# Pooled attention and a max-out MoE in one program: loads without a wait for an earlier load, and a new order of all engines and loads

## The chip, the core and the metric

The kernel runs on one core of a Trainium2 chip. TensorE (PE), ScalarE (ACT), VectorE (DVE) and GpSimd (POOL) each work through their own instructions in program order; SyncE (SP) issues nearly all of the DMAs, also in order, and 16 DMA engines carry them out. The metric is the device time of one execution in microseconds, the median of several.

## What is computed

```python
def _attn_ref(q, k, v):                       # 8 batches, 8 heads, 1152 positions, head size 64
    q_pool = q.reshape(B, H, S // 2, 2, D).mean(axis=3)
    scores = 1.0 / np.sqrt(D) * np.matmul(q_pool, k.transpose(0, 1, 3, 2))
    scores = scores - np.max(scores, axis=-1, keepdims=True)
    attn = np.exp(scores)
    attn = attn / (np.sum(attn, axis=-1, keepdims=True) + 1e-09)
    return np.matmul(attn, v)

def _moe_ref(x, w1, w2, w_out):               # x: 4608 tokens x 512; w1, w2: 512 x 1024; w_out: 1024 x 512
    g = np.maximum(x @ w1, x @ w2)
    return g @ w_out
```

The attention's output, heads side by side, is the `x` of the second part. Inputs and output are float32; the kernel multiplies in bfloat16.

## The kernel before

The 64 heads go in 32 pairs of two; a pair's q, k and v are three loads of 576 KB each. For each pair q is pooled and cast (`cast_q`, L435, on POOL), k is cast (`cast_k`, L405, POOL), v is cast and given a column of ones (`cast_v`, L445, POOL). k and q are turned so that the head size lies on the partitions: for pairs 0 to 4 on PE with a copy by DVE (`ktrans_pe`, L552 and L568; `qtrans`, L533 and L540), from pair 5 on k by a DMA transpose that SP issues (`ktrans`, L475), and q by eight small transposes on DVE (`qtrans_dve`, L485).

Scores come in 324 groups of 512 columns for both heads of a pair (`scores`, L302, on PE, into a pair of PSUM banks); ACT takes the exponent of each group (`exps`, L317; 336 instructions, since some groups are split where a buffer turns). A pair has 10.125 groups, so pair 3 begins in group 30, pair 4 in group 40, pair 6 in group 60. The product with v (`av_jobs`, L621 and L636, letter A) has eight steps a pair with a few more for the remainders, and DVE divides by the sums (L651, L654). The result is turned into `xT`.

The MoE uses max(a, b) = relu(a - b) + b. So the kernel forms `wd` = w1 - w2 on POOL, in eight halves of quarters (`w_diff`, L506), and the fused weight `w21` = w2 w_out on PE (`w_job`, L593), for which w2 is cast and turned and w_out is cast on DVE (`w_cast`, L498). The steps of relu(x wd) are `h_jobs` (L760, and L771 or L775 for the way out of PSUM), those of the output are `p_job` (L803, and L809 or L812). All of these are the letters 0 and 1. The first of them, the fused weight's, begin as soon as its weights are there; then come the first that read `wd`.

The order of the work is written out by hand as a string of letters, one letter a step, that a loop passes to `step`; it fixes the order on each engine and, with S for scores and E for exponents, how far the engines are apart. `BANKS` names the PSUM banks in that order. `LOADS` is the order of the loads (letter l takes the next one on SP; four small pieces of k of pair 0 and two of q of pair 0 come first, two of them on ACT's queue), `W_CASTS` that of the weight casts (letter c), `W_DIFFS` that of the halves of `wd` (letter d; the pair is quarter and half). In `LOADS` ("w", 0, c) is quarter c of w2, ("w", 1, c) of w1 and ("w", 2, c) of w_out; each is 512 KB.

Every step names what it reads and writes, and `Plan` puts in the semaphore waits that follow. A load waits for its buffer: there are three for each of q, k and v. From exponent 40 on it also waits for the exponent two groups back (`pace`). And by `BEHIND` it waits for an earlier load:

```python
        def behind():

            n = issued[0]
            issued[0] += 1
            back = [d for at, d in BEHIND if at <= n]
            return [f"ld{n - back[-1]}"] if back else [], [f"ld{n}"]
```

With `BEHIND = ((14, 3),)` the load at place 14 on SP (counted from 0) and all later ones wait until the load three places ahead has landed. `load_k`, `load_q`, `load_v` and `w_load` call it.

Of the kernel before, what the change touches and what calls it, by code (L numbers as in the profile page):

```python
# [116 lines left out]
def bass_funnel_attn__then__act_maxout2_kernel(  # L117
# [68 lines left out]
    BANKS = (
        "0124605424023623462032424660232342630240624702402064202420472042646264246024604640164604264126402406"
        "0240260240246304260346204040640606062061262062062402740264062402406402640642704260202402402406401640"
        "6460462056204620462046042164206204620620426026402602602602604604614646046046024604604204620420642040"
        "6406406742064264264206520640260462620620162062046206240620206204230642042042424126426046046045620642"  # L190
        "6024062046206206206206412640246056046206404024024026423236042642042626260262626426454526420642064206"
        "2454"
    )

# [1 line left out]
    with ctx:  # L196
# [230 lines left out]
        def cast_q0(i, lo, hi):  # L427
            op("DVE", lambda e: e.tensor_tensor(
                qpf[i][:, lo:hi, :], qraw[i][:, lo:hi, 0, :], qraw[i][:, lo:hi, 1, :], ALU.add),
                r=[f"qraw0.{lo}" if i == 0 else f"qraw{i}"], w=[f"qp{i}.{int(hi == QU)}"],  # L430
                cost=0.14 + (hi - lo) * 0.07, tag=("cq", i))
# [59 lines left out]
        def w_cast(part, ct, eng):  # L491
            n = 2 if part else 1
            src = (wof if part else w2f)[:, ct * n:(ct + 1) * n, :].rearrange("p a b -> p (a b)")
            dst = (wo if part else w2b)[:, ct * n:(ct + 1) * n, :].rearrange("p a b -> p (a b)")
            r = [f"wof{ct}" if part else f"w2f{ct}"]
            w = [f"wo{2 * ct}", f"wo{2 * ct + 1}"] if part else [f"w2b{ct}"]
            if eng == "DVE":
                op("DVE", lambda e: e.tensor_reduce(dst, src.unsqueeze(2), AX.X, ALU.max),  # L498
                   r=r, w=w, cost=1.21, tag=("wc", part, ct))
# [459 lines left out]
        for c in (
            "luFFlulllfyKQklgfbSkKEFlgFKSgESyFFlKEFgQSbESlFkSFEFFKlEySFSgESlqFFEFQlSbEFkSQElbKvSEgSlESceAAEATcESA"  # L960
            "EAhlkSaSEaASclEKAEglSAEcSAElvSaTaEhElTcSAESlAhAEScAElSSAcEAAlAqESa0a00aE0la0ScAE0SldQEaa00bSd0lEXSj0"
            "00ESvTl0h0E00eS4SlEAAkAEAlSa1ad1E1S1SEl1q1S1E1Kl1g1qE1S1SE1lQkrAEbArSdtAErArSE11avlEa1S5AElSdArESSrA"
            "dArEArSAEkAlaAaSEaAdatAESaXadjXEjSjSEXq0jl00jE0S0qr0E0lSr01rE11e41Sl1E1Sk1r10Er005St0ESv00r0ESSr0rvE"
            "lA4AAEASqalSaEAArAErAlSrSEEaAeaAArxAErSSaAEaAklrAAErS1at1ak1E1r0Sr0xE0r0Sr11E1rS1r0E050Sl0E0q0SrS0tE"
            "r01r10Er0eS0r0E0r0Skr0lE0r1S0r0E0rlSv0r1E14S11El1S1oSE1oAAEASAkEAaAlaSAEtAvSa1aE1SxS11ES111E1111ES11"
            "l1ESq5AAEAlSrSoEAroArAESrkSArEAaAalAEAaAaSvaaEtaSSrXEqArAjAEAjSrle00Ea0aS0rSE0lr0vSr0E1r01rlE114S11E"
            "1S1rSEA5AlvAEASr0E0ta0Eva0SrSE00xe00SE4AAkAESSlAEAaAaAEAlSa1aE1Sx000E0Sk11E0lS11E11S50qlE00tS00ESer0"
            "0rSE00rS0rE00r00Er0l0qSrSE0r01l1r0E14S11E1l1SroSE1r1o11roSErAoArAtEkArAAaaAArq1ESaa1E1Sx001r001E1r0S"
            "1rE0l001rS141E1rS1r1ES5AAEvAAroSSrvoESAlAAEvAaAaAlEAaAkaSa000SaEt0a000011114Ee111S111115E1S111Xl5EvS"
            "j00j0ESl0qSE0000SEl4AAAEArSSaEAaArAlqEArS1a1taE11rSESrE1e1xrS1r1EA5AAEASla0kaE0Sr00rSEq0l0r0SEr0ArAl"  # L970
            "E4SAAESr11aE1a1Srx1ESr11r1SEt5qAAAEArSe0aE0a0Slr0SEkr0S0r0E0lrS0r0E0r0Sl0rE0000ES0S0Er0tArAEArArS0aE"
            "0aq0Srx10Er1S14k1E1S11EroS1rSo1E1oAAoEvAAS1vElSAAlEAvAaSa1ESalAaAAEASa1aE1taS1rXvE1rS1j11Ej1eSrl11rE"
            "11qrSS5EAlAAkEAroS0a0oEa0S0rS0ErAAlAEASa0a0E0l0S4x00E0qSE0r00E0trSA4eAEAArS1a1Ea1k1Sr11ESr1lSr1E5AAA"
            "lEArS1a1Ea11Srx00E10S1l1E1S500tE0Sq0rS0Er00r0e0ESr00rSEl0kr00r0E0rS0l0ES00SE0A4AAEAAaAoaAoASaoSqaE11"
            "x11SESkr11t1rE11rE11rE1SrS1E1r11r1SEr11S1E1S11E1A5AEvAASoSvESlAAoAEvAaAaAElAaAa0Sa0a0E0taS00r0000E04"
            "e0Sx000r0E11141vS1x1E11r100500Sr11qE1Sr01lr110E1rS050E0Sl0r0E0SS0l0E0S0r0EArAArEAArlAkaAaArSE0etEa0a"
            "S0r0SE0rxS0rq0EA4AAEASkao1aE11o1SSE11lS11EA5AAElASa1aE1Sx0r00E0rS1rt0E0er0Sr0E1S4111ESl1r0q0E500S0lE"
            "0SrS0r0EA4lAAEAAAaaAASa1aESlk1Sx1r1ES1r11Ert11r11Er1qSSr1E1rArAEvAS1E11klS11El11vS1E1S1lvA5ESAAEAoAa"
            "oSaSESaAtaArAEArq00Ea0aSa00rExSv0r00ErS0xe0r0E0rSSr0kl0E0S00E0Sl00E0S00El0A4AEAAAaoSaSEoArAtArE00Ea0"
            "0aeS00rxE1111r00qS411E1111151S1k1E1r1Sl00500ESr000SrEl0A4AAEArSla1aE1S1S1EAAAEAlSa1aE1tSrS1rq1E1r1x1"  # L980
            "1rESSre11Er11rSk1Elr11S1E11Sl1E1A5AAEASaoSaEAoAAoEAoSa0a0tEq00rSESr0E00rx00k040E0AArvAArSrSvElArArAE"
            "AvaAaAAaAaSaSaE00a001x14E11S11E1x11Sv511E100S1SE0r1t11r0ES0500E0eSr00Er00SrSE0r00r0SEr0S00E0S00E0004"
            "0E00S0E0oS00oSE4AAAEAAaAaAeAAaEAaAAxAaAaAASa0aES0x00SE1000E0S411E1S11E111500S0E00S11E1S11E1S10E50S00"
            "E0S10E0Se10E00S00E0S00E0S00E10S41E11S11EoS11o1E1oSSo1E1AAEAAAaAaAAAaAaAxAAAAAaAaAAaAa1a1a1a11X1j11j1"
            "11111900001111111150000111o080110091o110000008101110191101000018111009101110000080101111191100000001"
            "001111910000000011111111110001000800110000o008001o11o00010181111Z9ZZZZZoZZoZZZZZZmZZZZzzZZZZZZZZZZmZ"
            "ZZZZZZzZzmzz"
        ):
            step(c)
# [52 lines left out]
```

## Time and profile before

| what | value |
|---|---|
| median of 3 runs | 365.27 us (364.27 to 365.68) |
| profiled execution | 362.49 us, span 360.8 us |
| PE clock granted, mean | 0.999 |
| loads of q, k, v: median from issue to landing | 6.2, 6.5, 5.8 us |
| DMA packets on SP's queue | 75856, 83.15 MB |

The profile is one execution on the chip. Its views name an engine, a line, the operation, and what is written and read; an idle time in front of an instruction carries the name of what ended it (`[1.91 <-PE ps L302]`: idle for 1.91 us until the matmul of line 302 was done). Matmuls are pipelined, so two that follow one another overlap in these lists, and the time from start to start is what one takes.

### The profile page before, as it was taken

How to read it: one execution, taken by the hardware profiler on the slowest of the kernel's cores; microseconds unless marked ns; L12 is line 12 of the kernel's file. 1: busy time of each engine (PE TensorE's matmuls, PEld its weight loads, DVE VectorE, ACT ScalarE, POOL GpSimd, SP SyncE). 2: the span in 40 equal slices, each digit the busy share in tenths (PEclk: the TensorE clock that was granted, in tenths of full speed). 3: DMA queues.
4: the chain of work that ended last, by engine and by line, in shares of the span. 5: the costliest groups of instructions: out<-in, count | busy, mean ns of one | idle time of the engine just before them, and what ended most of it. 6: DMA issues, size and time to landing. Idle time of an engine off the chain costs nothing.

```text
span 360.8 us, 13815 instructions
## 1 busy us (share of the span) xinstructions
PE 347.0 (96%) x6178; PEld 218.6 (61%) x6178; DVE 230.0 (64%) x472; ACT 314.0 (87%) x354; POOL 151.7 (42%) x136
## 2 busy tenths in 40 slices
PE   8888989999899999999999999999999999999996
PEld 6554564755655576556665576556575757448753
DVE  3587378992984985986886677785686875324001
ACT  5997979999999899999999889989999797892431
POOL 2623798562754444546444264326544531010000
PEclk9999999999999999999999999999999999999999
DMA  8999999999999989999999979999999972112215
GB/s 265 407 308 324 328 287 319 292 265 295 315 275 242 354 187 307 228 317 193 211 336 314 200 202 301 195 325 244 262 251 225 277 120 60 31 23 55 60 29 148
DMA packets 76699, 84.55 MB, mean 234 GB/s; under 512 B 48480, under 2 KB 49760, under 8 KB 76640
## 3 DMA queue, kind: packets, MB, share of 16 engines
q1 hardware_dynamic: 75856, 83.15, 88.2%
q8 instruction: 48, 0.79, 0.9%
q10 hardware_dynamic: 784, 0.52, 0.5%
q14 instruction: 11, 0.09, 0.1%
HBM read 62.91 MB, written 9.44 MB: 201 GB/s over the span
## 4 chain that ended last, share of the span: by engine, by line
PE 76%; DMA 12%; ACT 6%; DVE 2%; SPq 2%; issue 1%; POOL 1%; DVEq 0%; POOLq 0%
PE ps L803 23%; PE ps L621 17%; PE ps L302 16%; PE ps L760 15%; ACT et L317 6%; DMA kraw<-in_k_dram 5%; DMA qraw<-in_q_dram 3%; PE ps L636 3%; PE ps L846 1%; DMA stage<-in_moe_w_dram 1%; DMA stage<-in_moe_w_out_dram 1%; DMA vraw<-in_v_dram 1%; DVE qpT L485 1%; POOL qp L435 1%; SPq L346 1%
## 5 line engine op out<-in xcount | busy, mean ns | idle before, releaser
L317 ACT ACTIVATE et<-ps 128x1024 bf16<-128x1024 f32 (+1 forms) x336 | 302.5, 1019 | 18.6 <-PE ps L302 14.1
L302 PE MATMUL ps<-qpT,kT 64*128 64x256 bf16 (+7 forms) x1162 | 117.5, 283 | 4.8 <-DVE qpT L540 1.7
L485 DVE STREAM_TRANSPOSE qpT<-qp 32x288 bf16<-32x288 bf16 x216 | 101.3, 469 | 14.5 <-PE ps L302 6.2
L760 PE MATMUL ps<-xT,wd 64*128 64x512 bf16 (+3 forms) x832 | 81.2, 311 | 0.2
L302 PEld LDWEIGHTS ps<-qpT,kT 64*128 64x128 bf16 x1162 | 48.2, 94 | 52.4 <-ACT et L317 10.7
L803 PE MATMUL ps<-wo,stage 64*128 64x512 bf16 x544 | 76.4, 376 | 0.0
L435 POOL TENSOR_TENSOR qp<-qraw 128x576 bf16<-128x576 f32 x30 | 42.2, 1406 | 67.5 <-DMA qraw<-in_q_dram 67.5
L621 PEld LDWEIGHTS ps<-vE,et 128*128 128x128 bf16 x1728 | 54.8, 97 | 13.7 <-ACT et L317 8.9
L621 PE MATMUL ps<-vE,et 128*128 128x65 bf16 x1728 | 60.5, 193 | 0.5 <-ACT et L317 0.3
L771 DVE TENSOR_SCALAR stage<-ps 128x1024 bf16<-128x1024 f32 (+3 forms) x41 | 39.7, 968 | 20.7 <-PE ps L760 20.3
L760 PEld LDWEIGHTS ps<-xT,wd 64*128 64x128 bf16 x832 | 35.6, 94 | 22.3 <-PE ps L760 1.9
L405 POOL TENSOR_SCALAR kbf<-kraw 128x1152 bf16<-128x1152 f32 x31 | 35.8, 1153 | 31.1 <-DMA kraw<-in_k_dram 29.1
L803 PE MATMUL ps<-w,xT 64*128 64x512 bf16 x272 | 40.8, 377 | 0.0
L803 PEld LDWEIGHTS ps<-wo,stage 64*128 64x128 bf16 x544 | 26.4, 94 | 20.6
L445 POOL TENSOR_SCALAR vE<-vraw 128x1152 bf16<-128x1152 f32 x24 | 27.4, 1154 | 21.4 <-PE ps L636 10.7
L809 DVE COPY stage<-ps 128x1024 f32<-128x1024 f32 x14 | 17.1, 1224 | 22.9 <-PE ps L803 22.8
L654 DVE TENSOR_TENSOR xnat<-ps,rc 128x256 bf16<-128x256 f32 (+2 forms) x71 | 27.6, 397 | 2.0
L651 DVE RECIPROCAL rc<-ps 128x4 f32<-128x4 f32 (+2 forms) x64 | 11.6, 181 | 25.8 <-PE ps L621 25.2
L468 POOL TENSOR_SCALAR stage<-et 128x1152 bf16<-128x1152 bf16 x14 | 16.1, 1153 | 28.1 <-ACT et L317 28.1
L621 PE MATMUL ps<-stage,et 128*128 128x65 bf16 x576 | 19.8, 193 | 0.4 <-issue 0.4
L621 PEld LDWEIGHTS ps<-stage,et 128*128 128x128 bf16 x576 | 18.2, 97 | 3.2 <-issue 3.1
L803 PEld LDWEIGHTS ps<-w,xT 64*128 64x128 bf16 x272 | 12.5, 94 | 8.8 <-DVE stage L771 0.2
(55 smaller groups left out, 155.7 us busy)
## 6 DMA issues: line engine op xcount, KB each, us to landing
vraw<-in_v_dram SPq DMA_DIRECT2D x32, 576.0 KB, 5.8
kraw<-in_k_dram SPq DMA_DIRECT2D x31, 576.0 KB, 6.5
qraw<-in_q_dram SPq DMA_DIRECT2D x31, 576.0 KB, 6.2
...
```

Source lines behind the costliest of these rows:

```text
L302: last = e.matmul(ps[:, h, col:col + hi - lo], kT[i % 3][rows(h), t, :], qpT[i % 3][rows(h), lo:hi], start=True, stop=True)
L317: op("ACT", lambda e: e.activation(et2[:, :, c:c + z - a], ps[:, :, a - g * W:z - g * W], EXP, scale=scale), r=[f"b{m}", f"b{m + 1}"], w=w ...
L405: op("POOL", lambda g: g.tensor_scalar(kbf[s][:, :, :, :].rearrange("p t h d -> p h t d"), kraw[r][:, :, :, :], 1.0, 1.0, ALU.mult, ALU.mu ...
L435: op("POOL", lambda g: g.tensor_tensor(qpf[s][:, :, :], qraw[r][:, :, 0, :], qraw[r][:, :, 1, :], ALU.add), r=[f"qraw{r}"], w=[f"qp{s}.0", ...
L445: return g.tensor_scalar(vE[r][:, :, :, 0:D].rearrange("p t h d -> p h t d"), vraw[s][:, :, :, :], 1.0, 1.0, ALU.mult, ALU.mult)
L485: op("DVE", lambda e: e.transpose(view[dst:dst + 32, :, 32 * pb:32 * pb + 32], qpf[s][src:src + 32, :, 32 * db:32 * db + 32]), r=[f"qp{s}. ...
L621: last = e.matmul(fb[m][:, at * 66:at * 66 + 65], et[:, a:a + P], vE[vs][:, t, half, 0:65], start=(t == 0), stop=(t == NT - 1))
L654: todo.append(evac_op("DVE", lambda e, m, z=z, at=at, num=num, dst=dst: e.tensor_tensor(dst, a(m)[z, at:at + num, 0:D], rc[k][z, at:at + n ...
L760: last = e.matmul(fb[m + k][:, 0:size], wd[z, ct, (f0 + k) * P:(f0 + k + 1) * P], xT[z, ct, n0:n1], start=(turn == 0 and ct == 0), stop=(t ...
L771: return e.tensor_scalar_max(gT[:, f0:f0 + 2, g0:g0 + size], wide[m // 2][:, :, 0:size], 0.0)
L803: last = e.matmul(fb[m + k][:, :], lhs, rhs, start=(turn == 0 and j == 0), stop=(turn == 1 and j == NC_ + NF - 1))
L809: return e.tensor_copy(osb2[:, o:o + 2, :], wide[m // 2][:, :, :])
```

## The change

`BEHIND` becomes empty, so no load waits for another one to land; the waits for buffers and exponents stay. The loads, the weight casts, the halves of `wd`, the PSUM banks and the order of all steps are replaced by others. No step is added or taken away: both strings have 2712 letters, and the same number of each. The loads' order differs up to about pair 16, and the order of the steps mostly up to the same place; behind it single letters have moved by a few places.

```diff
@@ -153,27 +153,27 @@
     X_PE = (0, 1, 2, 3, 7, 11, 15, 31)
     HCUTS = (0, 512, 1024, 1152, 1664, 2048, 2304, 2816, 3072, 3456, 3968, 4096, 4352, 4608)
     W_ORDER = (1, 2, 0, 3)
-    W_CASTS = ((0, 1), (0, 3), (0, 0), (0, 2), (2, 0), (2, 1), (2, 2), (2, 3))
-    W_DIFFS = ((3, 0), (3, 1), (1, 0), (2, 0), (2, 1), (0, 0), (0, 1), (1, 1))
+    W_CASTS = ((0, 1), (0, 0), (0, 2), (2, 1), (2, 0), (2, 2), (2, 3), (0, 3))
+    W_DIFFS = ((3, 1), (0, 1), (1, 0), (2, 0), (3, 0), (0, 0), (1, 1), (2, 1))
     W_DIFFS_DVE = ()
     W_CASTS_POOL = ()
     W_PAIRS = (0, 2)
-    BEHIND = ((14, 3),)
+    BEHIND = ()
     FILL = 28
     FILLS = 16
     PACE = 2
     PACE_FROM = 40
     FOUR = 1
     LOADS = (
-        ("k", 0, 0, 2, "ACT"), ("k", 0, 4, 6, "ACT"), ("q", 0, 0, 4), ("k", 0, 2, 4), ("k", 0, 6, 9),
-        ("q", 0, 4, 9), ("k", 1), ("q", 1), ("q", 2), ("k", 2), ("v", 0), ("w", 0, 1), ("w", 0, 3),
-        ("k", 3), ("w", 0, 0), ("w", 0, 2), ("v", 1), ("w", 2, 0), ("w", 2, 1), ("w", 2, 2), ("q", 3),
-        ("w", 2, 3), ("w", 1, 3), ("v", 2), ("w", 1, 2), ("k", 4), ("w", 1, 1), ("q", 4), ("q", 5),
-        ("k", 5), ("v", 3), ("w", 1, 0), ("k", 6), ("q", 6), ("q", 7), ("k", 7), ("v", 4), ("v", 5),
-        ("q", 8), ("k", 8), ("k", 9), ("k", 10), ("q", 9), ("v", 6), ("k", 11), ("v", 7), ("k", 12),
-        ("q", 10), ("v", 8), ("q", 11), ("v", 9), ("v", 10), ("v", 11), ("k", 13), ("k", 14), ("q", 12),
-        ("v", 12), ("q", 13), ("v", 13), ("k", 15), ("q", 14), ("v", 14), ("k", 16), ("v", 15),
-        ("q", 15), ("q", 16), ("v", 16), ("q", 17), ("k", 17), ("v", 17), ("q", 18), ("k", 18),
+        ("k", 0, 0, 2, "ACT"), ("k", 0, 4, 6, "ACT"), ("k", 0, 2, 4), ("q", 0, 0, 4), ("k", 0, 6, 9),
+        ("k", 1), ("q", 0, 4, 9), ("q", 1), ("q", 2), ("k", 2), ("v", 0), ("w", 0, 1), ("w", 0, 0),
+        ("v", 1), ("w", 0, 2), ("k", 3), ("w", 2, 0), ("w", 2, 1), ("w", 2, 2), ("w", 2, 3), ("w", 0, 3),
+        ("q", 3), ("w", 1, 3), ("k", 4), ("q", 4), ("v", 2), ("k", 5), ("w", 1, 0), ("v", 3), ("k", 6),
+        ("q", 5), ("w", 1, 1), ("w", 1, 2), ("k", 7), ("q", 6), ("v", 4), ("k", 8), ("q", 7), ("v", 5),
+        ("q", 8), ("q", 9), ("v", 6), ("q", 10), ("v", 7), ("v", 8), ("k", 9), ("v", 9), ("q", 11),
+        ("v", 10), ("k", 10), ("v", 11), ("k", 11), ("k", 12), ("v", 12), ("k", 13), ("v", 13),
+        ("k", 14), ("q", 12), ("q", 13), ("v", 14), ("q", 14), ("v", 15), ("q", 15), ("k", 15),
+        ("q", 16), ("k", 16), ("v", 16), ("q", 17), ("k", 17), ("v", 17), ("q", 18), ("k", 18),
         ("v", 18), ("q", 19), ("k", 19), ("v", 19), ("q", 20), ("k", 20), ("v", 20), ("q", 21),
         ("k", 21), ("v", 21), ("q", 22), ("k", 22), ("v", 22), ("q", 23), ("k", 23), ("v", 23),
         ("q", 24), ("k", 24), ("v", 24), ("q", 25), ("k", 25), ("v", 25), ("q", 26), ("k", 26),
...
@@ -184,11 +184,11 @@
         "wwhhhhpphhhhpphhhhhhhhpphhhhpphhhhphhhhpphhhhphhhhphhhhpphhhhhhhhhphphh"
     )
     BANKS = (
-        "0124605424023623462032424660232342630240624702402064202420472042646264246024604640164604264126402406"
...
+        "0101010102460625640647672606422026342046203406402462046206202024016240260420402406520462060526026046"
...
@@ -957,33 +957,33 @@
                  "m": ("Z", 0), "4": ("0", 0), "5": ("1", 0), "6": ("2", 0), "7": ("3", 0),
                  "8": ("0", 1), "9": ("1", 1), "+": ("2", 1), "-": ("3", 1)}
         for c in (
-            "luFFlulllfyKQklgfbSkKEFlgFKSgESyFFlKEFgQSbESlFkSFEFFKlEySFSgESlqFFEFQlSbEFkSQElbKvSEgSlESceAAEATcESA"
-            "EAhlkSaSEaASclEKAEglSAEcSAElvSaTaEhElTcSAESlAhAEScAElSSAcEAAlAqESa0a00aE0la0ScAE0SldQEaa00bSd0lEXSj0"
-            "00ESvTl0h0E00eS4SlEAAkAEAlSa1ad1E1S1SEl1q1S1E1Kl1g1qE1S1SE1lQkrAEbArSdtAErArSE11avlEa1S5AElSdArESSrA"
-            "dArEArSAEkAlaAaSEaAdatAESaXadjXEjSjSEXq0jl00jE0S0qr0E0lSr01rE11e41Sl1E1Sk1r10Er005St0ESv00r0ESSr0rvE"
-            "lA4AAEASqalSaEAArAErAlSrSEEaAeaAArxAErSSaAEaAklrAAErS1at1ak1E1r0Sr0xE0r0Sr11E1rS1r0E050Sl0E0q0SrS0tE"
-            "r01r10Er0eS0r0E0r0Skr0lE0r1S0r0E0rlSv0r1E14S11El1S1oSE1oAAEASAkEAaAlaSAEtAvSa1aE1SxS11ES111E1111ES11"
-            "l1ESq5AAEAlSrSoEAroArAESrkSArEAaAalAEAaAaSvaaEtaSSrXEqArAjAEAjSrle00Ea0aS0rSE0lr0vSr0E1r01rlE114S11E"
-            "1S1rSEA5AlvAEASr0E0ta0Eva0SrSE00xe00SE4AAkAESSlAEAaAaAEAlSa1aE1Sx000E0Sk11E0lS11E11S50qlE00tS00ESer0"
...
+            "ulFFluFFlFFlFFFlffklykKlQgKbgSFESlFkKKEggSFlSEyFFQEblSyFESSSlEFqKEgSlkEQSbQElKbvgESSlSEcSElAecAEAAlT"
+            "aEaAvAhSlEScSAAElaTakEShTlEhKSgSElSAcESlEcSEAEAlAcSEA00cl0E00S0E00lSc00E0SAlEq0aSa0a0E0a0lSd4SEQAlAE"
+            "bkAASaTaElqhSKESg11le1E1S11ESvl1S1EQk1lb1E11Sdt1E1SS11EvA5AAEAkSlaSaEAAtqAEASaESaAEdrArAESrSdrEXrAjd"
+            "ESrlSrErdAAElAaSakXaESaAljAdEAjSaXaElSdjXt1jE1Sj0q0E00S0E0Ser00r1E1lS4v11E1S1rSklE0500E0qS0lrSE0r0Ar"
+            "AElArArS0aESaAlvA4tAEASEeaSEaSArxAErAqArSEaAaAArEAvrS1la1Ea1Sr1x0E0r1Sr1E1rqS1rl00E50S00E0lSr00Er00S"
+            "rSlE0rvS0r00Er00ler00E0rSSrq0El0r10r1E114Slk1E11SroS1ErtAArAEAAoaSaq1ESArAAEr1aSa1E1rxSSr1k1E1r11rSE"
+            "t1r11r1ES111ES5AAEvASoSEAovAlAESSvAEAlaAaAEAaAaSlaSaESarXElAerAjAEAjSr0lv0EaSa00r1E1rlSk0r0E0rS0t1rE"
+            "1kS411E11S5SEAAlAEASa0aE0t0ESe0SE00x00ES4AAEASkSElAAaAaEAAlSa1aE1Sx000E0Sk11E0Sl11E11S50lE0Sq0t00ES1"
...
```

Places in the new `LOADS` on SP, counted from 0: v of pair 0 is 8, the last quarter of w_out 17, q of pair 4 22, q of pair 5 28, w1's quarters 3, 0, 1 and 2 are 20, 25, 29 and 30. In the old one: v of pair 0 is 8, the last quarter of w_out 19, q of pairs 4 and 5 are 25 and 26, w1's quarters 3, 2, 1 and 0 are 20, 22, 24 and 29. In the old string the first step that reads `wd` stands behind 51 score groups and 52 exponents, in the new one behind 52 and 53.

More of the change, by code (lines that the diff above doesn't have):

```diff
@@ L186, in bass_funnel_attn__then__act_maxout2_kernel @@
     BANKS = (
-        "0124605424023623462032424660232342630240624702402064202420472042646264246024604640164604264126402406"
[L188 to L191, printed above, removed]
+        "0101010102460625640647672606422026342046203406402462046206202024016240260420402406520462060526026046"
+        "2402024026426520642506240202602602604670404604604264126402604264640624062064126402424624646464067406"
+        "4046042614260462046246240364026024602604206406240640640640642642652626426426402642642062406206420626"
+        "4264264520642642642604360420640246460460146046024604620460402406450264064064646142642062062067240264"
+        "2460240624024024024026402402460426142604620204204204624545062406462402026026026406454506402640264206"
         "2454"
@@ L965, in bass_funnel_attn__then__act_maxout2_kernel @@
-            "r01r10Er0eS0r0E0r0Skr0lE0r1S0r0E0rlSv0r1E14S11El1S1oSE1oAAEASAkEAaAlaSAEtAvSa1aE1SxS11ES111E1111ES11"
-            "l1ESq5AAEAlSrSoEAroArAESrkSArEAaAalAEAaAaSvaaEtaSSrXEqArAjAEAjSrle00Ea0aS0rSE0lr0vSr0E1r01rlE114S11E"
-            "1S1rSEA5AlvAEASr0E0ta0Eva0SrSE00xe00SE4AAkAESSlAEAaAaAEAlSa1aE1Sx000E0Sk11E0lS11E11S50qlE00tS00ESer0"
-            "0rSE00rS0rE00r00Er0l0qSrSE0r01l1r0E14S11E1l1SroSE1r1o11roSErAoArAtEkArAAaaAArq1ESaa1E1Sx001r001E1r0S"
-            "1rE0l001rS141E1rS1r1ES5AAEvAAroSSrvoESAlAAEvAaAaAlEAaAkaSa000SaEt0a000011114Ee111S111115E1S111Xl5EvS"
@@ L970, in bass_funnel_attn__then__act_maxout2_kernel @@
[L970 to L984, printed above, removed]
@@ new lines, in bass_funnel_attn__then__act_maxout2_kernel @@
+            "0e1rE0Sr10Er0qSr10Er00Sr0E0r0Sr00Er0Sq0r1E141S1E11rSo1SEroArAtAErAArAoAaaAo1rES1aE1a1Srx00001ErS1r10"
+            "E00r10Sr11E141Sr1ESrA5AvEAASroSvESlAAoAEvAaAaAEAalAaSaSaE1111a1l11111115E0e00011S1100E00l5S400vEXSj0"
+            "lEjS0S0ESlq000EA4AAlEkASaSaEAtrAqArEASr11Eak1a1SrxESE1r1e1r1SEt5AAAEArS0aE0a0Sr0lSErSq00r0E0rlA4AEAS"
+            "AElrS1a1aE11rxS1r1ESr11SrlEAk5AAEAleSa0atE0Sr00r0ESqSr00Er00r00Er0Sr0l0ESrSk00E00lS0Er0tArAEArArS0aE"
+            "0a0Srx11Er0S141Eq1S11Er1o1Srko1ESoAAovEAAS1vElSAAlEAvAaSa1ESalAaAAEASla1aE1at1SrXE1reS1j11Ej1Srv11rE"
@@ new lines, in bass_funnel_attn__then__act_maxout2_kernel @@
+            "11rSqSl5EAAAEAkroS0a0oEa00SrS0ErlAAAEASal0a0E0Sx4000E0SEq0r0t0E0rSA4eAEAArS1a1Ea11kSr11lE1r1SrSE5AAl"
+            "AEArS1a1Ea1l1Sr0x1E0S01E11S500tE0Sq0r0ESr0Sr0E0e0rS0lrE00rk00rSE0lr000E00SSE0A4AAEAAaAoaAoASao1aqE1S"
+            "xS1r1ES1kr1t1Er11Er11Er1SSr1E1r11r11E11SSE1S111EA5AvAEASoSvESlAAoAEvAaAaAElAaAa0Sa0a0E0taS00r0000E04"
+            "e0Sx000r0E11141Sv1x1E11r100500SrSE11r1q00lr11E11rS050E0Sl0r0E0SS0l0E0S0r0EArlAArEAArAaAelaArSE0Ea0ka"
+            "S0lr00ExSrS0r0EqA4tAAEASak1oaE11o1SSE111S1EA5AqAEAlSa0aE0SxSr00E1r10rt0E1erS0r0E1S411E1S1r0E0l500S0k"
@@ new lines, in bass_funnel_attn__then__act_maxout2_kernel @@
+            "E0SrlS0r0EA4AAElAAAaaAASa1aES1x1S1Er1S1rt1E1r11qr1E1rSS1rE1krAArEASv1E111Svl1E11lS1v1ES1A5ElSAAEAoAa"
+            "oSaSESaAtaArAEAr0v0Ea0aSa00rEx0qSr00Er0Sx0re0E0rSSr0k0E0l0S0E0000El00S0ES4AlAAEAAoaSaoSEArtAArE00Ea0"
+            "0aeS00rxE1111rS11qrE11111510011141Sk00E005Sl0000rSEA4AAElrASr1E1aSa1l1SES111ElAAAEASal1aE1tSr11r1ESe"
+            "rSx11rE1Srq11Er1Sr11Er1kS11E1lA5AAEqASao0a0E00oS0oSEAoAAEASa0a0Et0SrE0040E0Sx0k00rES0rAA4EvAASrSvESl"
+            "rArAAErvAAaAaEAaAaS1a1Ea11aS1r1xE11S511E10x10vS0ErS1t1r110Er0eS500E0S0r0E0r0SrSE0rS0r00E000SE0S00E00"
@@ L987, in bass_funnel_attn__then__act_maxout2_kernel @@
+            "040E00S0E0oSS0o0EA4AAeAAaAaAAAaEAaEAAxAaAaAASaSaE00x00SE1110E01S0E0S4111E1115S1E0000S1E0S111E1S500E0"
+            "S00E0e0SSE0S000E0000E0S00E0S411E11S1oES11o11Eo11o1SSEAAAEAAaAaAAAaAaAxAAAAAaAaAAaAa1a1a1a111X1j11j11"
+            "11111900001111111150000111o180000191o110000008100111019000008001110000008001111019011000080101111111"
+            "10000080011111111111111911001111o1090o1101o000101110900000000000Z8ZZZZZoZZoZZZZZZmZZZZzzZZZZZZZZZZmZ"
             "ZZZZZZzZzmzz"
```

2 lines of the change are left out of this document (removed).

## The prediction

> **What bounds the kernel now.** I read the page first, then the busy time by stretches, then the chain of waits of the first 60 us, and last the timelines of ScalarE and GpSimd there.
>
> ```profile
> span 360.8 us, 13815 instructions
> PE 347.0 (96%) x6178; PEld 218.6 (61%) x6178; DVE 230.0 (64%) x472; ACT 314.0 (87%) x354; POOL 151.7 (42%) x136
> ```
> ```profile
> 0.00:20.00 20.00, 16.83 (x304) 11.14 (x305) 9.46 (x19) 16.12 (x19) 8.55 (x17) 1.00 0.93 338
> 20.00:40.00 20.00, 17.17 (x365) 10.89 (x366) 14.65 (x24) 17.77 (x21) 8.26 (x8) 1.00 0.92 311
> 40.00:60.00 20.00, 17.48 (x334) 10.40 (x330) 12.48 (x29) 17.70 (x21) 17.74 (x16) 1.00 1.04 300
> 80.00:100.00 20.00, 18.86 (x394) 12.68 (x392) 12.24 (x30) 19.30 (x22) 10.53 (x9) 1.00 1.08 308
> 100.00:340.00 240.00, 239.30 (x4314) 152.22 (x4310) 161.42 (x333) 218.23 (x247) 93.93 (x78) 1.00 0.89 217
> ```
>
> The columns are the stretch, its length, the busy time of PE, PE's weight loads, DVE, ACT and POOL, PE's clock, the share of the DMA engines and GB/s. From 100 to 340 us PE is busy for 239.3 of 240 us, so no load that lands earlier can gain anything there by itself. Before 60 us PE has 8.5 us of idle time and ACT 8.4, because the exponents, PE's score groups that feed them, and data that is still on its way set the pace in turn. What time can be had lies there, and it reaches the end only by letting the later, PE-bound part begin sooner.
>
> ```profile
> 6.91 12.27 DMA kraw<-in_k_dram
> 19.20 4.54 DMA vraw<-in_v_dram
> 23.76 5.20 DMA stage<-in_moe_w_out_dram
> 28.98 5.23 DMA stage<-in_moe_w_dram
> 34.22 5.14 DMA kraw<-in_k_dram
> 39.38 5.37 DMA qraw<-in_q_dram
> 44.82 1.41 POOL qp L435
> ```
> ```profile
> SPq L370 <- DMA kraw<-in_k_dram: 9.8, 1, 9.8
> ```
>
> The chain runs through loads alone from 6.9 to 44.8 us. Each piece begins when the one before it has landed: that is the rule of `BEHIND`, by which the fifteenth and every later load on SP's queue waits for the load three places ahead. At its beginning the rule holds SP for 9.8 us.
>
> ```profile
> 25.75 7.44 ACT L317 ACTIVATE et<-ps 128x1024 bf16<-128x1024 f32 x8 [0.32 <-PE ps L302]
> 35.09 10.21 ACT L317 ACTIVATE et<-ps 128x1024 bf16<-128x1024 f32 x11 [1.91 <-PE ps L302]
> 47.55 3.08 ACT L317 ACTIVATE et<-ps 128x512 bf16<-128x512 f32 x4 [2.25 <-PE ps L302]
> 32.95 1.22 DVE L498 TENSOR_REDUCE wo<-stage 128x1024 bf16<-128x1024 f32 x1 [1.57 <-DMA stage<-in_moe_w_out_dram]
> 34.22 0.61 PE L593 MATMUL ps<-wo,xT 64*128 64x512 bf16 x4 [1.68 <-DVE wo L498]
> 44.82 1.40 POOL L435 TENSOR_TENSOR qp<-qraw 128x576 bf16<-128x576 f32 x1 [0.31 <-DMA qraw<-in_q_dram]
> 46.26 0.47 DVE L485 STREAM_TRANSPOSE qpT<-qp 32x288 bf16<-32x288 bf16 x1 [3.21 <-POOL qp L435]
> 47.12 0.39 PE L302 MATMUL ps<-qpT,kT 64*128 64x256 bf16 x4 [1.34 <-DVE qpT L540]
> ```
>
> After its first exponents ACT stops three times up to 60 us, for 0.32, 1.91 and 2.25 us, 4.48 us in all. The second stop is the last quarter of w_out: it lands at about 32.9 us, its cast follows, PE stands 1.68 us before the fused-weight product, and the next score group is behind it. The third is q of pair 5, landed at about 44.8 us: DVE stands 3.21 us before that pair's first transpose; the copy of pair 4's q is queued behind it, and pair 4's first scores wait 1.34 us more for that copy.
>
> **The change part by part.** Both orders hold the same steps, letter for letter in count, and by the 100th score group both have issued 76 attention-value steps and 127 or 128 MoE steps. So the change is worth what it takes from the time to that group, apart from the switches below. I sum against the profiled execution (362.49 us, its span 360.8). It lies 2.78 us under the 365.27 us of the median, and I carry the difference over to the median.
>
> *The three stops: -4.48 us, all of it if nothing comes in their place.* To date the loads I need their rate without the rule. In this kernel the loads ahead of the fifteenth already run so:
>
> ```profile
> 8.99 1.15 POOL L405 TENSOR_SCALAR kbf<-kraw 128x1152 bf16<-128x1152 f32 x1 [2.84 <-DMA kraw<-in_k_dram]
> 15.19 1.16 POOL L445 TENSOR_SCALAR vE<-vraw 128x1152 bf16<-128x1152 f32 x1 [0.64 <-DMA vraw<-in_v_dram]
> 19.26 1.15 POOL L405 TENSOR_SCALAR kbf<-kraw 128x1152 bf16<-128x1152 f32 x1 [1.80 <-DMA kraw<-in_k_dram]
> ```
> ```profile
> 8.00:12.00 4.00, 3.58 (x68) 1.81 (x68) 1.96 (x4) 4.00 (x5) 1.20 (x2) 1.00 1.04 417
> 28.00:32.00 4.00, 4.00 (x73) 2.41 (x67) 3.13 (x6) 4.00 (x5) 1.41 (x1) 1.00 0.92 321
> ```
>
> These three casts begin as their loads land: k of pair 1, v of pair 0 four loads later, k of pair 3 three after that. That is seven loads in 10.27 us, 1.47 us each, with the last three (two of them weights) at 1.35. Under the rule, from 23.76 to 44.82 us, twelve loads take 21.06 us, 1.75 each. The rates beside them are 417 and 321 GB/s. So I take 1.47 us, and 1.35 and 1.75 as ends. In the new order the last quarter of w_out is nine loads after v of pair 0: 15.2 + 13.2 = 28.4 us in place of 32.9. q of pair 4 is 14 after it: 35.8 us, and q of pair 5 is 20 after it: 44.6, but its transposes now stand behind the copy of pair 4's q. Both long stops fall with microseconds to spare.
>
> [...]
>
> *What is late next: w1 for the first MoE product, +1.5 us.* The new order puts two w1 quarters at places 29 and 30 (counted from 0; v of pair 0 is 8). The second lands at 15.2 + 22 x 1.47 = 47.5 us. Only then can POOL make that quarter's first half of `wd`, and behind it in POOL's new order stand two halves, the cast of k of pair 7, and two halves more, the last of them the same quarter's second half.
>
> ```profile
> 52.31 1.15 POOL L405 TENSOR_SCALAR kbf<-kraw 128x1152 bf16<-128x1152 f32 x1
> 53.42 2.50 POOL L506 TENSOR_TENSOR wd<-stage,xT 128x512 bf16<-128x512 f32 x2
> 56.19 1.04 PE L760 MATMUL ps<-xT,wd 64*128 64x512 bf16 x8
> ```
>
> Five halves at 1.27 and a cast of 1.15 are 7.5 us: 55.0. PE begins the MoE product at 56.19 us now. The new order has it one score group later (10.21 / 11 = 0.93 us), and the 4.48 us come off: 52.6; its third step, which reads that quarter, comes a group later: 53.5. PE arrives 1.5 us early and stands, with the scores queued behind it. At 1.35 us a load the halves are done at 52.4 and it costs nothing; at 1.75 they are done at 61.2 and it costs 7.7. I take 1.5, by the nearest row.
>
> *Fewer switches of PE: -0.3 us.* The new order changes 130 times between attention-value and other steps, the old one 142 times.
>
> ```profile
> 108.33 0.65 PE L302 MATMUL ps<-qpT,kT 64*128 64x384 bf16 x8
> 108.91 1.53 PE L621 MATMUL ps<-vE,et 128*128 128x65 bf16 x45
> 110.38 0.39 PE L302 MATMUL ps<-qpT,kT 64*128 64x512 bf16 x2
> 110.60 0.59 PE L760 MATMUL ps<-xT,wd 64*128 64x512 bf16 x4
> ```
>
> Two score groups before a run of such steps take 0.58 us from start to start, against 0.22 for one beside other work: 0.14 a switch, or 1.7 us for twelve. Ten of them lie before the 80th group, where ACT sets the pace and covers PE. Two lie after it: 0.3 us. Without the cover the ten would count too; ends -1.7 and 0.
>
> *At nothing:* the first piece of q moves one place back on SP's queue.
>
> ```profile
> 0.80 0.41 SPq L358 DMA_DIRECT2D qraw<-in_q_dram  x1
> 3.78 0.43 DVE L428 TENSOR_TENSOR qp<-qraw 128x256 bf16<-128x256 f32 x1 [2.71 <-DMA qraw<-in_q_dram]
> 4.86 0.31 PE L533 MATMUL ps<-ident,qp 64*64 64x64 bf16 x8
> ```
>
> Its cast ends at 4.21 us, and PE, still turning k, takes it up at 4.86. That covers a place on the queue (0.41 us of issuing); uncovered it costs 0.4. The regrouped casts and transposes of pairs 6 to 17 have six or more exponents of about 0.93 us between load and cast nearly everywhere; I take 0, from -0.7 (the page of the first 100 us leaves 0.7 us of ACT idle time between 80 and 100) to +2.25, one more stop of the largest size seen. SP loses the rule's wait instructions, and its transposes and stores move ahead in time; they now stand behind more queued loads.
>
> ```profile
> kT<-kbf SPq DMA_TRANSPOSE x27, 6.0
> ```
>
> A kT transpose lands in 6.0 us; the new order leaves twelve or more exponents, 11 us, between its issue and its first use. Three more loads ahead of it, 4.4 us, still fit.
>
> Sum: -4.48 + 1.5 - 0.3 = -3.3 us. The profiled execution goes to 359.2, the median to 362.0 us.
>
> **The rivals.**
>
> *All of it is had.* If loads land every 1.40 us or faster, the halves of `wd` are ready as PE arrives: -4.48 - 0.3 = -4.8, 360.5 us. For it: the last three loads at 1.35. Against: the seven at 1.47.
>
> [...]
>
> *Slower.* If the 1.75 us a load are what DMA gives whenever packets of all kinds are queued, and not the rule's doing, then the new order has put w1 too late: the halves come at 61.2, PE loses 7.7 where it gained 4.48, +3.2 - 0.3: 368.2 us. It decides from 1.61 us a load on. For it: the DMA share is 0.92 to 1.04 with the rule too, so its engines do not look idle. Against: 321 GB/s at share 0.92 beside 417 at 1.04.
>
> **How the numbers follow.** The forecast has 0.40, its own range 360.8 to 364; all of it had 0.13; the time moved away 0.22; slower 0.25. About 0.5% (1.8 us) is what a measurement of this kernel can tell from no change. Under 363.4 lie nearly all of the forecast, the first rival and a little of the second: 0.52. The rest of these is 0.23, and slower by more 0.25. The range goes from 359.0 (all of it, with the 0.7 us and more switches) to 368.2, the slower rival's price.
>
> **What would show it.** Right: no stop of ACT over 1 us between 24 and 48 us; SP's w1 loads landed by 48 us; one new stop of PE of 1 to 2 us before the MoE product's `wd` at 52 to 55 us, released by POOL; from 100 us on the same full PE, some 3 us earlier. Wrong: loads 1.6 us apart or more after 20 us, POOL's last half of `wd` after 57 us, a wait of the scores for kT or for a transposed q after 60 us, or PE idle after 100 us.

## The result and the profile after

| | median | range, runs | ratio to before, 95% interval |
|---|---|---|---|
| before, first comparison | 365.44 us | 362.82 to 366.74, 6 | |
| after, first comparison | 360.28 us | 359.25 to 361.30, 6 | 0.9869 [0.9831, 0.9906] |
| before, a later comparison on another chip | 363.74 us | 361.08 to 367.92, 17 | |
| after, the same | 360.53 us | 359.63 to 361.16, 7 | 0.9923 [0.9895, 0.9950] |

The changed kernel is faster. It gave nearly the same time twice; it is the kernel before that moved, and in three comparisons with 17 to 29 executions each its median was 363.5 to 363.7. So by the medians the gain is 5.2 us in the first comparison and 3.2 in the larger one; by the ratios, which leave out the one slow execution of 367.92 us, it is 4.8 and 2.8. The profiled execution of after took 360.07 us.

The first lines of its page and the busy time by stretches, with the columns as before:

```profile
span 358.3 us, 13762 instructions
PE 346.9 (97%) x6178; PEld 219.1 (61%) x6178; DVE 229.2 (64%) x472; ACT 314.3 (88%) x354; POOL 151.5 (42%) x136
```
```profile
0.00:20.00 20.00, 16.07 (x286) 11.47 (x287) 8.53 (x18) 14.16 (x17) 8.24 (x17) 0.91 0.91 336
20.00:40.00 20.00, 17.88 (x370) 10.84 (x369) 15.10 (x23) 19.36 (x23) 9.30 (x8) 1.00 1.04 397
40.00:60.00 20.00, 18.67 (x363) 11.19 (x360) 12.94 (x31) 20.00 (x24) 19.66 (x19) 1.00 1.14 290
80.00:100.00 20.00, 19.76 (x404) 12.81 (x402) 15.26 (x36) 19.80 (x23) 9.41 (x8) 1.00 0.97 253
100.00:340.00 240.00, 239.39 (x4316) 152.68 (x4314) 157.18 (x327) 216.85 (x245) 92.80 (x77) 1.00 0.84 212
```

From 20 to 60 us ACT is busy for 39.36 of 40 us, where it had 35.47, and the loads run at 397 GB/s in the stretch from 20 to 40 us, where they ran at 311. From 100 us on PE is as full as it was. In the first 20 us it is the other way round: ACT has 14.16 us of work there, and had 16.12.

The timelines of ACT, of POOL and of PE (start, duration, what ended the idle time before):

```profile
6.92 3.77 ACT L317 ACTIVATE et<-ps 128x1024 bf16<-128x1024 f32 x4 [2.17 <-PE ps L302]
11.62 13.07 ACT L317 ACTIVATE et<-ps 128x1024 bf16<-128x1024 f32 x14 [0.92 <-PE ps L302]
24.97 11.50 ACT L317 ACTIVATE et<-ps 128x1024 bf16<-128x1024 f32 x13 [0.29 <-PE ps L302]
36.68 24.10 ACT L317 ACTIVATE et<-ps 128x1024 bf16<-128x1024 f32 x27 [0.20 <-PE ps L302]
```
```profile
35.32 1.41 POOL L435 TENSOR_TENSOR qp<-qraw 128x576 bf16<-128x576 f32 x1 [0.28 <-DMA qraw<-in_q_dram]
...
44.68 1.41 POOL L435 TENSOR_TENSOR qp<-qraw 128x576 bf16<-128x576 f32 x1
46.05 4.96 POOL L506 TENSOR_TENSOR wd<-stage,xT 128x512 bf16<-128x512 f32 x4
50.98 1.15 POOL L405 TENSOR_SCALAR kbf<-kraw 128x1152 bf16<-128x1152 f32 x1
52.09 2.50 POOL L506 TENSOR_TENSOR wd<-stage,xT 128x512 bf16<-128x512 f32 x2
```
```profile
54.96 0.61 PE L760 MATMUL ps<-xT,wd 64*128 64x512 bf16 x4
55.40 0.38 PE L302 MATMUL ps<-qpT,kT 64*128 64x384 bf16 x4
55.62 0.61 PE L760 MATMUL ps<-xT,wd 64*128 64x512 bf16 x4
```

The stops of 1.91 and 2.25 us are gone. q of pair 4 is cast as it lands at 35.3 us; q of pair 5 is there before POOL gets to it at 44.68. The last halves of `wd` end at 54.59 us, and PE begins the MoE product at 54.96 with no idle time before it. But the first exponent starts at 6.92 us instead of 5.99, and there is a stop of 0.92 us at 11.62 that this profile of before did not have (its second profile, below, has one of 0.72 us at 10.44).

The start of the n-th exponent, counted off in the traces, dates gain and loss. Each column is a mean over the profiled executions of that kind; "no 3" stands for kernels without a wait or with one for the load six places ahead, which the experiments bring in.

| exponent | before (2) | old order, no 3 (4) | new order, no 3 (3, after among them) |
|---|---|---|---|
| 1 | 6.24 us | 6.00 | 6.93 |
| 30 | 32.73 | 32.97 | 34.68 |
| 60 | 64.66 | 60.15 | 61.65 |
| 100 | 101.77 | 96.85 | 98.30 |
| span | 361.6 | 357.4 | 358.7 |

From exponent 30 to 60 the kernel before takes 31.9 us, and both orders take 27.0 to 27.2 without the wait. That is the gain. The new order comes to exponent 30 1.7 us later than the old one, and that is a loss; 1.3 us of it are there by exponent 10 (15.85 against 14.55 us).

### The profile page after: what moved, and what is told of

It is laid out like the page before. It is cut to its first block, busy times and chain, and to the rows that moved or that the text cites. A ratio compares the mean times of both kernels' runs of the same rounds, so it can differ in the third digit from the quotient of the medians.

```text
span 358.3 us, 13762 instructions
## 1 busy us (share of the span) xinstructions
PE 346.9 (97%) x6178; PEld 219.1 (61%) x6178; DVE 229.2 (64%) x472; ACT 314.3 (88%) x354; POOL 151.5 (42%) x136
## 4 chain that ended last, share of the span: by engine, by line
PE 74%; ACT 17%; DMA 4%; DVE 3%; issue 1%; SPq 1%; POOL 0%
PE ps L803 21%; ACT et L317 17%; PE ps L621 16%; PE ps L302 16%; PE ps L760 15%; DMA qraw<-in_q_dram 4%; PE ps L636 2%; DVE qpT L485 2%; PE ps L846 1%; PE ps L593 1%; POOL qp L435 0%; SPq L346 0%; DVE stage L809 0%; PE ps L552 0%; DVE xnat L654 0%
## 5 line engine op out<-in xcount | busy, mean ns | idle before, releaser
L302 PE MATMUL ps<-qpT,kT 64*128 64x256 bf16 (+7 forms) x1162 | 115.5, 285 | 3.5 <-ACT et L317 1.7
L302 PEld LDWEIGHTS ps<-qpT,kT 64*128 64x128 bf16 x1162 | 48.5, 94 | 50.6 <-ACT et L317 11.8
L803 PE MATMUL ps<-wo,stage 64*128 64x512 bf16 x544 | 75.2, 376 | 0.0
L760 PEld LDWEIGHTS ps<-xT,wd 64*128 64x128 bf16 x832 | 35.3, 94 | 21.2 <-PE ps L760 1.0
L803 PE MATMUL ps<-w,xT 64*128 64x512 bf16 x272 | 39.6, 377 | 0.0
L445 POOL TENSOR_SCALAR vE<-vraw 128x1152 bf16<-128x1152 f32 x24 | 27.2, 1153 | 23.6 <-PE ps L636 21.1
L651 DVE RECIPROCAL rc<-ps 128x4 f32<-128x4 f32 (+2 forms) x64 | 11.8, 184 | 30.6 <-PE ps L621 30.1
L809 DVE COPY stage<-ps 128x1024 f32<-128x1024 f32 x14 | 17.1, 1225 | 18.5 <-PE ps L803 18.3
```

Of the source, the lines that this page charges most:

```text
L302: last = e.matmul(ps[:, h, col:col + hi - lo], kT[i % 3][rows(h), t, :], qpT[i % 3][rows(h), lo:hi], start=True, stop=True)
L445: return g.tensor_scalar(vE[r][:, :, :, 0:D].rearrange("p t h d -> p h t d"), vraw[s][:, :, :, :], 1.0, 1.0, ALU.mult, ALU.mult)
L760: last = e.matmul(fb[m + k][:, 0:size], wd[z, ct, (f0 + k) * P:(f0 + k + 1) * P], xT[z, ct, n0:n1], start=(turn == 0 and ct == 0), stop=(t ...
L803: last = e.matmul(fb[m + k][:, :], lhs, rhs, start=(turn == 0 and j == 0), stop=(turn == 1 and j == NC_ + NF - 1))
L809: return e.tensor_copy(osb2[:, o:o + 2, :], wide[m // 2][:, :, :])
```

## The experiments

### The wait alone

```diff
-    BEHIND = ((14, 3),)
+    BEHIND = ()
```

The edit is made to the kernel before, with nothing else changed. The kernel before itself ran beside it.

> The kernel before, unchanged, for a second profile and the spread of its executions. The first profiled execution lay 2.8 us under the median of the runs. If that was one early execution, this profile lies at about 365 us and shows where the other 3 us go: either ACT's stops at exponents 31 and 42 are longer than 1.91 and 2.25 us, or there are more of them. If the time outside the span differs, the span is 361 us again and the stops are the same.

> The old order of loads and steps, with the wait for the load three places ahead taken away alone. Theory (the wait made the loads slow, 1.75 us each, and the loads made the stops): loads land every 1.4 to 1.5 us, the last quarter of w_out (11 loads after v of pair 0) at 31 in place of 32.9 us, q of pair 5 (18 after it) at 41 in place of 44.8; the stop of 1.91 us nearly goes, that of 2.25 us mostly, about 4 us less: 361.5 us. Rival (the new order makes the gain): the stops stay within 0.5 us, 365 us. Second rival (the order was made for the wait, and loads issued early get in the way of DMA transposes): over 366 us.

The kernel before gave 363.01 us against 363.47 (ratio 0.9984 [0.9954, 1.0014]). Without the wait it gave 359.26: 0.9873 [0.9826, 0.9921], or 4.2 us. ACT in the second profile of the kernel before, and then in the one without the wait:

```profile
10.44 24.00 ACT L317 ACTIVATE et<-ps 128x1024 bf16<-128x1024 f32 x27 [0.72 <-PE ps L302]
35.77 10.22 ACT L317 ACTIVATE et<-ps 128x1024 bf16<-128x1024 f32 x11 [1.33 <-PE ps L302]
49.02 0.60 ACT L317 ACTIVATE et<-ps 128x512 bf16<-128x512 f32 x1 [3.04 <-PE ps L302]
```
```profile
21.75 39.21 ACT L317 ACTIVATE et<-ps 128x1024 bf16<-128x1024 f32 x44 [0.30 <-PE ps L302]
```

The two long stops come back in the second execution of before, as 1.33 and 3.04 us. Without the wait 44 exponents follow one another from 21.75 to 60.96 us. By the DMA records q of pair 4 lands at 39.5 us there, where it landed at 43.0, and 22 loads from 16.33 to 47.10 us take 1.40 us each. Nothing but `BEHIND` differs, so the wait is the cause of both stops.

### The same wait in the new order

```diff
-    BEHIND = ()
+    BEHIND = ((14, 3),)
```

> The new order with the old wait put back alone. Theory: loads from place 14 on land every 1.75 us, the w1 quarter at place 30 at 52 in place of 46.9 us, the last half of wd some 5 us later than 54.6, PE stands there with the scores behind it, and the time is 364 to 366 us, no better than before. Rival (the order makes the gain): 360 to 361 us.

368.69 us (367.61 to 369.87, 6 executions), 1.0141 [1.0097, 1.0185] of before. POOL, DVE, PE and ACT of this kernel:

```profile
50.10 1.40 POOL L435 TENSOR_TENSOR qp<-qraw 128x576 bf16<-128x576 f32 x1 [0.99 <-DMA qraw<-in_q_dram]
52.70 5.01 POOL L506 TENSOR_TENSOR wd<-stage,xT 128x512 bf16<-128x512 f32 x4 [1.21 <-DMA stage<-in_moe_w_dram]
57.68 1.16 POOL L405 TENSOR_SCALAR kbf<-kraw 128x1152 bf16<-128x1152 f32 x1
58.79 2.50 POOL L506 TENSOR_TENSOR wd<-stage,xT 128x512 bf16<-128x512 f32 x2
```
```profile
51.53 2.39 DVE L485 STREAM_TRANSPOSE qpT<-qp 32x288 bf16<-32x288 bf16 x5 [3.06 <-POOL qp L435]
53.93 0.42 DVE L733 COPY xT<-ps 128x512 bf16<-128x512 bf16 x1
```
```profile
54.42 0.39 PE L302 MATMUL ps<-qpT,kT 64*128 64x64 bf16 x4 [2.80 <-DVE xT L733]
```
```profile
54.85 1.02 ACT L317 ACTIVATE et<-ps 128x1024 bf16<-128x1024 f32 x1 [1.84 <-PE ps L302]
```

q of pair 5 now lands last before its use: POOL waits for it, DVE for POOL, a copy of `xT` stands behind five transposes on DVE, and PE waits 2.80 us for that copy. The halves of `wd` end at 61.29 us, but PE comes to their product only at 59.82 us and stands 0.19 us for the last of them: the stop that was expected before `wd` comes earlier, at q of pair 5. The time is above the 364 to 366 us expected. From exponent 30 to 60 this kernel takes 31.3 us, much as the kernel before does (31.9); another 2.08 us go at 127.9 us, where PE waits for a copy by DVE (L809) that stands behind ten transposes of q. Put back, the rule costs 8.2 us here (against 360.53 us on another chip), and 4.2 to 5.7 in the old order. This order has q of pair 5 two places later among the loads than the old one and the last quarter of w1 one; whether these places make it pay more was not tried.

### Six places instead of three

```diff
-    BEHIND = ((14, 3),)
+    BEHIND = ((14, 6),)
```

> The old order with the wait kept, but for the load six places ahead in place of three. Theory (three loads under way are too few to keep the DMA engines busy): with six the loads land every 1.45 to 1.5 us, both stops go, and the time is that of the old order without a wait: ratio 0.987 to 0.990. Rival (any wait for a landing costs, since SP stands still and transposes behind it come late): half of the gain or less, 0.993 or more.

357.31 us, 0.9838 [0.9807, 0.9870] of a kernel before of 363.58 us. So a wait for a load does no harm by itself in this kernel; what matters is how many loads are under way. By the DMA records 22 loads take 1.42 us each with six, and 1.40 (old order) or 1.43 (new) with no limit. With three they take 1.69, the first of them still ahead of the rule, and 1.75 by the chain in the prediction.

### The wait for `wd`: one w1 quarter a place later

```diff
-        ("q", 5), ("w", 1, 1), ("w", 1, 2), ("k", 7), ("q", 6), ("v", 4), ("k", 8), ("q", 7), ("v", 5),
+        ("q", 5), ("w", 1, 1), ("k", 7), ("w", 1, 2), ("q", 6), ("v", 4), ("k", 8), ("q", 7), ("v", 5),
```

The edit is made to the kernel after. No stop for `wd` was left to take away, so this one makes it come.

> The new kernel with its last w1 quarter one place later in the order of loads, behind k of pair 7, whose letter stands behind a kT transpose. Theory (a late w1 stops PE before the product with wd, one for one beyond the slack): the quarter lands at 50 to 51 in place of 46.9 us, POOL starts that quarter's first half 3 to 4 us later than 47.3, the last half ends at 57 to 58.5 in place of 54.6, PE stands 1.5 to 3 us there, and the time is 1.5 to 3 us over the new kernel's: ratio to before 0.991 to 0.995. Rival (there are several us of slack, the term was idle): no difference.

362.59 us, 0.9981 [0.9959, 1.0004] of before, some 2 us above the kernel after. Its POOL and PE:

```profile
50.60 3.74 POOL L506 TENSOR_TENSOR wd<-stage,xT 128x512 bf16<-128x512 f32 x3 [3.07 <-DMA stage<-in_moe_w_dram]
54.30 1.16 POOL L405 TENSOR_SCALAR kbf<-kraw 128x1152 bf16<-128x1152 f32 x1
55.42 2.49 POOL L506 TENSOR_TENSOR wd<-stage,xT 128x512 bf16<-128x512 f32 x2
```
```profile
55.19 0.39 PE L760 MATMUL ps<-xT,wd 64*128 64x512 bf16 x2
56.74 0.39 PE L760 MATMUL ps<-xT,wd 64*128 64x512 bf16 x2 [1.17 <-POOL wd L506]
```

The quarter lands at 50.5 us instead of 46.9, POOL ends at 57.91 instead of 54.59, and PE stands for 1.17 us in the middle of the first MoE steps, less than the 1.5 to 3 expected. Exponent 60 comes at 63.37 us, where it came at 61.51. The path that the prediction's second step describes is there, and the kernel after lies on its near side: there the last half is done at 54.59 us, and the third step, which reads it, begins at 56.07.

### The late start of the new order

`new_q_first` moves the second piece of q one place ahead in the kernel after. `new_start` also drops seven of the nine fillers (matmuls without use, letter F) at the head of the string, with their banks. `new_start_dve` also makes two halves of `wd` on DVE instead of POOL (their letters d become n).

```diff
-        ("k", 1), ("q", 0, 4, 9), ("q", 1), ("q", 2), ("k", 2), ("v", 0), ("w", 0, 1), ("w", 0, 0),
+        ("q", 0, 4, 9), ("k", 1), ("q", 1), ("q", 2), ("k", 2), ("v", 0), ("w", 0, 1), ("w", 0, 0),
```
```diff
-            "ulFFluFFlFFlFFFlffklykKlQgKbgSFESlFkKKEggSFlSEyFFQEblSyFESSSlEFqKEgSlkEQSbQElKbvgESSlSEcSElAecAEAAlT"
+            "ulFFlulllffklykKlQgKbgSFESlFkKKEggSFlSEyFFQEblSyFESSSlEFqKEgSlkEQSbQElKbvgESSlSEcSElAecAEAAlTaEaAvAh"
```

```diff
-    W_DIFFS = ((3, 1), (0, 1), (1, 0), (2, 0), (3, 0), (0, 0), (1, 1), (2, 1))
-    W_DIFFS_DVE = ()
+    W_DIFFS = ((3, 1), (0, 1), (1, 0), (2, 0), (1, 1), (2, 1))
+    W_DIFFS_DVE = ((3, 0), (0, 0))
```

> The new kernel with the second piece of q of pair 0 put back ahead of k of pair 1 in the order of loads, nothing else. Theory: that piece lands at about 7 in place of 9.6 us, ACT's stop of 0.92 us before exponent 5 goes, and the exponents run 0.9 to 1.1 us ahead of the new kernel up to 50 us. PE then reaches the first product with wd at 54 in place of 55.0 us, where the last half is done at 54.6 for its third step, so 0.5 to 1 us of it stays: 359.5 us. Rival: PE waits the whole of it out before wd, 360.3 us, no gain. If the stop stays, k of pair 0 or PE's fillers hold it.

> The new kernel with both of its changes at the start undone: the second piece of q of pair 0 ahead of k of pair 1 again, and seven of the nine filler steps ahead of the first transpose left out (fillers compute nothing of the output). Theory: the fillers held the first transpose of k, so the first exponent starts at 6.0 us as in the old order (new order: 6.7 to 7.3), 0.8 us sooner. The product with wd is reached that much sooner and has under 1 us to wait for the last half: 0.5 to 0.8 us of gain against the new kernel, ratio to before about 0.985. Rival: the first loads set the start; first exponent at 6.7 us or later.

> The same, and two of the eight halves of wd (the fifth and sixth) made by DVE in place of POOL. Theory (the last half of wd is the next thing late, by POOL's chain): POOL ends its last half 2.5 us sooner, and what the earlier start gains goes through whole: 0.5 to 1 us under new_start. Rival: PE arrives after the last half anyway, no difference, or DVE's two extra halves delay the copies out of PSUM: 0 to 1 us slower.

| kernel | first exponent | exponent 30 | ratio to before |
|---|---|---|---|
| after (two profiles) | 6.92, 7.26 us | 34.54, 34.61 us | 0.9869, 0.9923 |
| new_q_first | 7.28 | 36.40 | 0.9906 [0.9873, 0.9938] |
| new_start | 6.17 | 34.40 | 0.9958 [0.9927, 0.9988] |
| new_start_dve | 6.17 | 34.12 | 0.9993 [0.9963, 1.0024] |

None of the three gains anything. ACT in `new_q_first`, and then in `new_start`:

```profile
7.28 9.28 ACT L317 ACTIVATE et<-ps 128x1024 bf16<-128x1024 f32 x10 [2.77 <-PE ps L302]
17.93 3.77 ACT L317 ACTIVATE et<-ps 128x1024 bf16<-128x1024 f32 x4 [1.38 <-PE ps L302]
23.39 7.50 ACT L317 ACTIVATE et<-ps 128x1024 bf16<-128x1024 f32 x9 [1.69 <-PE ps L302]
```

```profile
6.17 1.94 ACT L316 ACTIVATE et<-ps 128x1024 bf16<-128x1024 f32 x2 [1.68 <-PE ps L301]
8.34 1.94 ACT L316 ACTIVATE et<-ps 128x1024 bf16<-128x1024 f32 x2 [0.23 <-PE ps L301]
11.15 5.75 ACT L316 ACTIVATE et<-ps 128x1024 bf16<-128x1024 f32 x6 [0.87 <-PE ps L301]
17.65 17.77 ACT L316 ACTIVATE et<-ps 128x1024 bf16<-128x1024 f32 x20 [0.76 <-PE ps L301]
```

In `new_q_first` the stop before exponent 5 is gone, as its theory says. Two others come in its place, of 1.38 us, where PE had waited for k of pair 2 (landed at 15.43 us, in after at 13.96), and of 1.69 us, with PE's clock at 0.50 up to 22.8 us (the last section). Its median of 360.55 us is that of the kernel after.

Without the fillers the first exponent comes 0.75 us earlier (6.17 us in both kernels, 6.62 to 7.28 in the six profiles of the new order that have them), though the first piece of q has the same place, so it was the fillers and not that place that made it late. But ACT stops for 0.87 and 0.76 us again, and by exponent 30 only 0.14 us is left. What `new_start` and `new_start_dve` lose against the kernel after lies far behind the start: they reach exponent 100 at 98.01 and 98.09 us, after at 98.16, and from there to the end of the span they take 262.5 and 262.4 us, after 260.2. Why is not settled. In the profile of `new_start` PE stands twice near 282 and 288 us for nothing that the profile shows, 1.37 us in all, and in that of `new_start_dve` once for 1.05 us:

```profile
282.65 0.50 PE L759 MATMUL ps<-xT,wd 64*128 64x384 bf16 x4 [0.57 <-issue]
...
288.03 1.49 PE L620 MATMUL ps<-stage,et 128*128 128x65 bf16 x44 [0.80 <-issue]
```

### Both orders on one chip

Four kernels on one chip: after, the old order without the wait, and both orders with six. The edits are those shown above; in the new order six is `BEHIND = ((14, 6),)` in place of `()`.

> The kernel after, unchanged, beside the three that follow on one chip. It is the measure for them: 0.987 of the kernel before (0.983 to 0.991) if the first comparison holds.

> The kernel before with BEHIND empty and nothing else changed, a second time, beside the kernel after on the same chip. Theory (removing the wait is the whole gain, the new order adds nothing to it): the same time as the kernel after within 0.4%, about 0.986 of the kernel before. Rival (the new order has a gain of its own that the first comparison on two different chips hid): the kernel after is faster than this one by 0.5% or more.

> The kernel before with the wait for the load six places ahead instead of three. [...] Rival (the first look was a lucky execution): equal to the one without the wait within 0.2%, or slower than it.

> The kernel after with the wait for the load six places ahead put back. Theory (depth six gives the same rate as no limit, 1.41 against 1.43 us a load): the time of the kernel after within 0.4%, so far below the 1.014 that three places gave in this order. Rival (the new order needs its loads as early as an unlimited queue issues them): 0.7% or more slower than the kernel after.

| | no wait | six places | three places |
|---|---|---|---|
| old order | 358.06 us, 0.9857 [0.9816, 0.9897] | 358.67 us, 0.9877 [0.9838, 0.9916] | 363.74 us (before) |
| new order | 360.53 us, 0.9923 [0.9895, 0.9950] | 361.46 us, 0.9930 [0.9905, 0.9955] | 368.69 us, 1.0141 (other chip) |

Six and no limit are alike in both orders; the better time of six on the other chip did not come again. Between the orders neither expectation held: the old one is 2.5 us faster without the wait, and 2.8 with six. Against the intervals that is a little more than chance. On two chips apart the first comparisons had shown no difference (0.9869 and 0.9873). With the 1.45 us at exponent 100 in the profiles I read it as a cost of the new order of 0 to 2.5 us, most likely about 1.5. The old order's ACT and the head of its copies on POOL:

```profile
21.09 39.52 ACT L317 ACTIVATE et<-ps 128x1024 bf16<-128x1024 f32 x44
```
```profile
36.19 1.15 POOL L405 TENSOR_SCALAR kbf<-kraw 128x1152 bf16<-128x1152 f32 x1
37.31 1.27 POOL L506 TENSOR_TENSOR wd<-stage,xT 128x512 bf16<-128x512 f32 x1
38.54 2.76 POOL L435 TENSOR_TENSOR qp<-qraw 128x576 bf16<-128x576 f32 x2
```

In the old order too q of pairs 4 and 5 is cast by 41.30 us as soon as the loads run at 1.4 us, without any new place for them. The rearrangement that was to let late loads land in time had nothing left to mend.

## Why the prediction came out as it did

Forecast 362.0 us, a gain of 3.3; measured 360.28 and 360.53, a gain of 5.2 and 3.2. Both times lie inside the stated range of 359.0 to 368.2, but just under the forecast's own 360.8 to 364 and at the price of the rival "all of it", 360.5; of the gains the larger comparison's is the forecast's. The number holds partly by luck: two of its terms were wrong against each other.

- **"The three stops: -4.48 us".** Right in cause, place and size. The wait's removal alone is worth 4.2 and 5.7 us in the medians of two chips, and 4.8 us between exponents 30 and 60. Loads came 1.43 us apart, with 1.47 taken from the seven loads ahead of the rule. The last quarter of w_out landed at 28.3 us (forecast 28.4), q of pair 4 at 35.2 (35.8), q of pair 5 at 44.3 (44.6).
- **"What is late next: w1 for the first MoE product, +1.5 us".** The dates hold: the quarter at 46.9 (47.5), the halves done at 54.59 (55.0). The stop did not come, since PE began the product not at 52.6 but at 54.96 us, and its third step not at 53.5 but at 56.07: the steps before it ran late. On the forecast's date for that third step the halves would have been 1.1 us late. The delayed quarter shows the mechanism, 3.3 us later on POOL and some 2 us at the end.
- **"At nothing".** This is the step that failed. The start was weighed by one place of q on SP, 0.4 us at most. The new start costs 0.9 us at the first exponent and 1.7 by exponent 30. That took the place of the +1.5 for `wd`, nearly to the size, and so the sum stood by luck. The string's first letters, fillers among them, had not been costed. What beside the fillers makes the first 30 exponents late stays open.
- **"Fewer switches of PE, -0.3".** Not seen and not tried by itself. From exponent 100 to the end of the span the three columns of the table take 259.8, 260.6 and 260.4 us, so a difference of this size is lost in theirs.
- **The rivals.** "All of it" needed 1.40 us a load; at 1.43 the halves were in time all the same, since PE came late, so its price was met and its reason was not. The time did not move into the wait for `wd`, which had a chance of 0.22: the loads came 1.43 us apart, at 397 GB/s from 20 to 40 us, and PE began that product with no idle time before it. The slower rival has a condition of 1.75 us a load and a date of 61.2 us for the halves. The new order with the rule met the condition (13 loads from the last quarter of w_out to the last of w1 take 23.55 us by the DMA records, 1.81 each) and gave 61.29 us for the halves. Its 368.69 us in all lie near the rival's 368.2, but not by the rival's path: PE stood 0.19 us for `wd`, not 7.7. And the 1.75 us are the rule's doing, which that rival denied.

Of the signs that were named, three were seen: no stop of ACT over 1 us between 24 and 48 us, w1 landed by 48, and PE full from 100 us on, with exponent 100 2.4 us earlier in the two first profiles and 3.5 in the means. The fourth, a stop of PE before `wd`, was not.
